# Second-layer weights four rows to a partition, first-layer columns at a step of four, five fetch buffers

## The chip, the core and the metric

The kernel runs on one core of a Trainium2 chip. The metric is the device time of one execution in microseconds. Before the change it is 216.29 us, the median of three runs (215.66 to 222.16).

## What is computed

Two layers follow each other. The first is an mLSTM cell: for 4 batches and 8 heads with a head size of 40, over 768 steps, with exponential input and forget gates that are kept stable by a running maximum `m`:

```
C = f_stab * C + i_stab * outer(v_t, k_t)
n = f_stab * n + i_stab * k_t
y_t = sigmoid(o_t) * (C @ q_t) / max(|n . q_t|, 1)
```

Its output, as 3072 rows of 320 values, goes into a mixture of 8 experts. Each row goes to one expert, and no row is dropped:

```
expert_idx = argmax(x @ w_gate);  gate_w = softmax(x @ w_gate)[expert_idx]
h = max(x_rows_of_e @ w1[e], 0)      # 320 -> 1024
y = gate_w * (h @ w2[e])             # 1024 -> 320
```

## The kernel before

**Recurrent stage.** The sequence of each batch is cut into 6 chunks of 128 steps, so there are 24 tiles, handled in one loop over `s` with an order that is written out by hand. A tile's rows are scored against the eight columns of `w_gate`, ranked, and scattered by GpSimd (`send`, L596) into a table `x_sorted` in device memory that is sorted by expert.

**Expert stage.** It starts in the last steps of the loop (at about 117 us in the trace) and takes the rest of the time. The rows of an expert are worked on in groups: a group of two tiles (256 rows) and a group of one tile (128 rows) for every expert, in the order of the list `order` (L824). Two groups, those of experts 0 and 1 with two tiles, are done early, while the buffers of the recurrent stage are still in place. Rows beyond the 384 of an expert go into five extra one-tile groups, whose expert is known only at run time. A loop of the same kind stands behind them for rows beyond these; it isn't entered where five extra groups are enough.

For a group, `turn` transposes its rows into `xT` (L253, L254), `layer1` computes the hidden values and applies the maximum with 0 (VectorE L286, ScalarE L288), and `layer2` computes the output `zp` (L293), copies it to `zo` (ScalarE, L298) and scatters it to the output rows (GpSimd, L300).

**Weights.** They lie in device memory as f32 and are cast to bf16 by the transfer itself, which GpSimd issues: `weights_whole` (L186) and `weights_half` (L193) for the first layer, `weights_out` (L200) for the second. All experts stay in two tiles, `w1_all` and `w2_all`. The program's transfers from GpSimd share eight completion semaphores in turn, so one waits until the eighth before it has landed.

**The layout that the change touches.** A block of 128 hidden values is one contraction of the second layer. Which 128 of the 1024 rows of `w2[e]` form a block is free, so long as the first layer computes the same hidden values in that block. With `j=2`, partition `p` holds the rows 2p and 2p+1 of a stretch of 256, which lie next to each other in device memory. Block `fb` then has every second hidden value, so the first layer reads the columns of its weights at a step of two. These lines say it:

```python
w2_all[:, e].rearrange("p e (a j) d -> p (e a) (j d)", j=2)            # L201
return fb // 2 * 256 + fb % 2                                          # L257
lhsT=w[:, c : c + 255 : 2], rhs=xT[:, db, :]                           # L282
```

The columns are the operand of the weight load (LDWEIGHTS), 24 of them a group: 8 at L271 over 64 partitions and 16 at L280 over 128.

**Fetches.** An extra group can't name its expert's weights when the program is built. So `fetch` (L808 to L813) copies them from `w1_all` and `w2_all` into buffers `wx1` and `wx2`, issued on SyncE's queue with the expert's number in a register. There are `XW` buffers of each; fetch number `x` is issued when group `i = 14 - XW + x` starts (L841 to L843). Since a fetch may read any expert, the first of them waits until all weights have landed.

**PSUM banks of the early groups.** The recurrent stage has six tags with one bank each (`tk`, `tq`, `sA`, `sB`, `dC`, `xt`) and one tag, `hp`, with two. `spots` (L624 to L629) says which bank the early expert groups use for what; a list is used in turn. Their outputs `zp` have the two banks of `hp`.

Of the kernel before, what the change touches and what calls it, by code (L numbers as in the profile page):

```python
# [19 lines left out]
def kernel(  # L20
# [37 lines left out]
    FL = DB - 1  # L58
# [10 lines left out]
    XU = 5  # L69
    NE = 2  # L70
    PE_ = 7
    XW = 4
    NV = 6
    NS = N + 128

# [89 lines left out]
    w2_all = big.tile([128, E, FB, Dm], BF16)  # L165
# [32 lines left out]
    def weights_out(e0, n):  # L198
        e = slice(e0, e0 + n)
        nc.gpsimd.dma_start(  # L200
            w2_all[:, e].rearrange("p e (a j) d -> p (e a) (j d)", j=2),  # L201
            moe_w2[e].rearrange("e (a p j) d -> p (e a) (j d)", p=128, j=2),
        )

    def apart(ins, group):
# [24 lines left out]
    def spot(kind, shape, dtype):  # L230
        i = turns[kind] = turns.get(kind, -1) + 1
        at = spots[kind][i % len(spots[kind])]
        if isinstance(at, tuple):
            tag, pool = at
            return pool.tile(shape, dtype, name=kind, tag=tag)[:]
        n = 1
        for m in shape[1:]:
            n *= m
        at = at[:, :n]
        return at.rearrange("p (a b) -> p a b", b=shape[2]) if len(shape) == 3 else at  # L240
# [13 lines left out]
        nc.vector.tensor_copy(g["xT"], tp)  # L254

    def column(fb):
        return fb // 2 * 256 + fb % 2  # L257

    def layer1(g, u):
        n = g["n"]  # L260
        per = 4 // n
        w, xT = g["w"][0], g["xT"]
        v = u // 2 * per
        if u == 0:
            g["h"] = spot("h", [128, FB, n * 128], BF16)
            g["hp"] = [spot("hp", [128, per, n * 128], F32) for _ in range(2 * n)]
            for k in range(HF):
                for a in range(2):
                    c = FL * F + column(k)
                    r = slice(64 * a, 64 * a + 64)  # L270
                    nc.tensor.matmul(  # L271
                        g["hp"][k // per * 2 + a][:, k % per, :], lhsT=w[r, c : c + 255 : 2], rhs=xT[r, FL + a, :],
                        start=(k % per == 0), stop=False, skip_group_check=True,
                    )
        a = u % 2
        hp = g["hp"][u]
        for i in range(per):
            for db in range(FL):
                c = db * F + column(a * HF + v + i)
                nc.tensor.matmul(  # L280
                    hp[:, i, :], lhsT=w[:, c : c + 255 : 2], rhs=xT[:, db, :], start=False, stop=(db == FL - 1),
                    skip_group_check=True,  # L282
                )
        dst = g["h"][:, a * HF + v : a * HF + v + per, :]
        if a == 0:
            nc.vector.tensor_relu(dst, hp)  # L286
        else:
            nc.scalar.activation(dst, hp, AF.Relu)  # L288
# [30 lines left out]
    with tc.tile_pool(name="ring", bufs=1) as ring_pool, \  # L319
# [301 lines left out]
        for i in range(1, NV):  # L621
            pads(i)
        early = [dict(e=e, n=NE, k=0, si=0, zp="zp") for e in range(2)]
        spots.update(  # L624
            hp=[(t_, ps1) for t_ in ("sA", "sB", "tk", "tq")], tp=[("dC", ps1)], zp=[("hp", ps2)],
            h=[kq[:, i].rearrange("p a h d -> p (a h d)").bitcast(BF16) for i in range(2)],
            xT=[kq[:, 2, a].rearrange("p h d -> p (h d)").bitcast(BF16) for a in range(2)],
            zo=[zo_e[:, i, :] for i in range(4)],
# [6 lines left out]
        for s in range(-3, NT):  # L635
# [55 lines left out]
            if s == NT - 5:  # L691
                weights_out(0, 1)
            if s == NT - 4:
                weights_in(1, 1)
            if s == NT - 3:
                weights_out(1, 1)
            if s == NT - 2:
                weights_in(2, 1)
        weights_whole(3)
        assert sent == NT - 4  # L700
        layer1(first, 0)
        xtrans(NT - 1)
        gate(P0)
        rank(P0, NT - 1)
        layer1(first, 1)
        place(P0)
        for t in (NT - 4, NT - 3):
# [3 lines left out]
        logits(P0 + 1, NT)  # L711
        choose(P0 + 1)
        layer1(first, 2)
        gate(P0 + 1)
        targets(1, 0)
# [8 lines left out]
        nc.vector.tensor_copy(tot[:], rt[P0 + 1]["tot"])  # L724
        weights_half(3)
        weights_out(2, 1)
        weights_out(3, 1)
        layer2(first, 0)
# [79 lines left out]
    def fetch(ex):  # L808
        wx1 = wk_pool.tile([128, FL * F + F // 2], BF16, name="wx1", bufs=XW)
        wx2 = wk_pool.tile([128, FB, Dm], BF16, name="wx2", bufs=XW)  # L810
        nc.sync.dma_start(wx1[:], w1_all[:, bass.ds(ex, 1), :].rearrange("p e b -> p (e b)"))
        nc.sync.dma_start(wx2[:].rearrange("p a b -> p (a b)"), w2_all[:, bass.ds(ex, 1)].rearrange("p e a b -> p (e a b)"))  # L812
        return wx1, wx2  # L813

    def expert_of(x):
        return nc.sync.value_load(xe[0:1, bass.ds(x, 1)], min_val=0, max_val=E - 1)
# [22 lines left out]
    for i, g in enumerate(groups):  # L839
        nw = g.get("e", E) + 3  # L840
        x = i - len(order) + XW  # L841
        if 0 <= x < XU:
# [21 lines left out]
    with tc.If(nx > XU):  # L864
        with tc.For_i(XU, nx, 1) as i:
            iv = wk_pool.tile([128, 1], F32, name="iv")
            nc.vector.tensor_copy(iv[:], invx[:, bass.ds(i, 1)])
            g = dict(n=1, w=fetch(expert_of(i)), apart=False)
# [36 lines left out]
```

## Time and profile before

The profile covers one execution with a span of 205.5 us on the one core, at a mean granted TensorE clock of 0.992.

| engine | busy us | share of the span |
|---|---|---|
| TensorE, matmuls | 184.8 | 90% |
| TensorE, weight loads (beside the matmuls) | 153.1 | 75% |
| VectorE | 125.5 | 61% |
| ScalarE | 117.0 | 57% |
| GpSimd | 142.0 | 69% |

| transfers | count | size of one, as written | median time from issue to landing |
|---|---|---|---|
| second-layer weights, GpSimd's queue | 8 | 640.0 KB | 8.7 us |
| first-layer weights, whole part | 8 | 512.0 KB | 10.6 us |
| first-layer weights, half part | 16 | 64.0 KB | 8.4 us |
| fetches of the extra groups, SyncE's queue | 10 | 640.0 KB | 7.0 us |

How to read it: matmuls are pipelined and their ends are modelled, so a TensorE that is 90% busy isn't at 90% of its peak. The sizes of cast transfers are those of the bf16 side; twice as many bytes are read. In the views of the trace a line names the source line, the engine, the operation, and the tiles as `written<-read`; `w_all` stands for `w1_all` and `w2_all`, `wx` for `wx1` and `wx2`. PEld is the weight load of TensorE; SPq is SyncE's queue.

### The profile page before, as it was taken

What the parts mean: (1) busy time and instruction counts of PE and PEld (TensorE: products, weight loads), DVE (VectorE), ACT (ScalarE), POOL (GpSimd) and SP (SyncE); (2) the same over time, 40 slices, a digit from 0 to 9 for tenths busy, and PEclk for the clock granted to TensorE, in tenths of its full rate; (3) what the DMA queues carried; (4) which work ended last, traced back from release to release, by engine and by line L of the source; (5) the groups of instructions that cost most, each with busy time, mean ns of one, the idle gap of its engine ahead of it and who ended that gap; (6) DMA issues with size and microseconds to landing.
All of it is one profiled execution on the core that took longest, in us unless ns stands there. A gap on an engine that the chain in (4) does not pass through costs nothing.

```text
span 205.5 us, 5756 instructions
## 1 busy us (share of the span) xinstructions
PE 184.8 (90%) x2055; PEld 153.1 (75%) x2055; DVE 125.5 (61%) x410; ACT 117.0 (57%) x273; POOL 142.0 (69%) x259
## 2 busy tenths in 40 slices
PE   1289999999999999999999999998998999999660
PEld 1166888888999989998888877666866877777450
DVE  7854757678777887879858774454853343433210
ACT  1457775878978988699584375343333342533320
POOL 6024779546486898978899978974437769898632
PEclk9999999999999999999999999999999999999996
DMA  7999999999999899999969998999999999999930
GB/s 137 197 190 192 208 225 193 190 226 206 217 172 212 165 188 185 199 185 192 199 93 280 254 222 188 122 210 249 234 233 217 228 263 273 393 378 389 366 133 23
DMA packets 116686, 44.32 MB, mean 216 GB/s; under 512 B 102506, under 2 KB 111725, under 8 KB 116656
## 3 DMA queue, kind: packets, MB, share of 16 engines
q1 hardware_dynamic: 105456, 25.34, 59.1%
q0 software_dynamic: 10736, 18.38, 40.4%
q8 instruction: 17, 0.28, 0.5%
q10 hardware_dynamic: 464, 0.21, 0.4%
q14 instruction: 13, 0.11, 0.1%
HBM read 39.30 MB, written 9.37 MB: 237 GB/s over the span
## 4 chain that ended last, share of the span: by engine, by line
PE 44%; DMA 21%; DVE 9%; POOL 8%; issue 7%; ACT 5%; SPq 4%; POOLq 1%; ACTq 0%; DVEq 0%
DMA w_all<-in_moe_w_dram 18%; PE hp L418 7%; PE hp L486 7%; PE tk L380 5%; PE dC L426 5%; PE sA L393 4%; PE tq L380 4%; PE xt L463 4%; PE sA L398 3%; POOL out_dram L300 3%; DMA wx<-w_all 2%; PE hp L438 2%; SPq L812 2%; POOL w_all L193 2%; POOL rest L309 2%
## 5 line engine op out<-in xcount | busy, mean ns | idle before, releaser
L286 DVE TENSOR_SCALAR h<-hp 128x512 bf16<-128x512 f32 x25 | 17.3, 692 | 35.2 <-PE hp L280 16.4
L288 ACT ACTIVATE h<-hp 128x512 bf16<-128x512 f32 x25 | 14.9, 597 | 25.5 <-PE hp L280 24.1
L596 POOL DMA_INDIRECT x_sorted<-x_all,slots x24 | 25.5, 1061 | 5.3 <-issue 3.1
L456 POOL TENSOR_TENSOR x_sb<-x_sb,den 128x320 f32<-128x320 f32 x23 | 16.7, 726 | 15.8 <-DVE den L454 15.3
L300 POOL DMA_INDIRECT out_dram<-zo,s_idx x20 | 19.9, 994 | 7.1 <-ACT zo L298 3.1
L293 PE MATMUL zp<-w_all,h 128*128 128x320 bf16 x160 | 24.0, 299 | 0.7 <-DMA w_all<-in_moe_w_dram 0.7
L293 PEld LDWEIGHTS <-h 128*128 128x128 bf16 x200 | 18.8, 98 | 7.1 <-DMA w_all<-in_moe_w_dram 0.9
L405 ACT CAST dB<-sB 128x512 bf16<-128x512 f32 x24 | 14.0, 584 | 14.0 <-PE sB L399 12.7
L280 PEld LDWEIGHTS <-w_all 128*128 128x128 bf16 x256 | 18.9, 98 | 3.7 <-issue 1.3
L298 ACT COPY zo<-zp 128x320 f32<-128x320 f32 x25 | 10.6, 425 | 18.4 <-PE zp L293 18.4
L418 PE MATMUL hp<-C_sb,qT 104*128 104x82 f32 x160 | 20.7, 272 | 0.1
L380 PE MATMUL tk<-ident,kq 128*104 128x128 f32 x96 | 16.7, 300 | 4.1 <-DMA kq<-in_k_dram 4.1
L280 PE MATMUL hp<-xT,w_all 128*128 128x128 bf16 (+1 forms) x224 | 20.1, 243 | 0.0
L418 PEld LDWEIGHTS hp<-C_sb,qT 104*128 104x128 f32 x160 | 19.4, 192 | 0.6 <-PE tq L380 0.3
L368 POOL CAST vAb<-vA 128x328 bf16<-128x328 f32 x24 | 11.0, 460 | 11.7 <-DVE vA L366 11.7
L465 ACT COPY xT<-xt 128x384 f32<-128x384 f32 x24 | 11.6, 482 | 12.4 <-PE xt L463 12.1
L406 POOL TENSOR_SCALAR_AFFINE_SELECT dB<-dB 128x512 bf16<-128x512 bf16 x24 | 16.5, 689 | 2.2 <-ACT dB L405 2.0
L426 PE MATMUL dC<-vA,kq 128*104 128x82 f32 x160 | 17.9, 255 | 0.0
L486 PE MATMUL hp<-wg_sb,xT 128*128 128x8 f32 x144 | 17.7, 256 | 0.0
L403 DVE TENSOR_TENSOR dA<-sA,cmask 128x512 bf16<-128x512 f32 x24 | 16.0, 667 | 1.9 <-PE sA L398 1.9
L486 PEld LDWEIGHTS hp<-wg_sb,xT 128*128 128x128 f32 x144 | 17.0, 192 | 0.0
L426 PEld LDWEIGHTS dC<-vA,kq 128*104 128x104 f32 x160 | 16.3, 172 | 0.0
(156 smaller groups left out, 454.8 us busy)
## 6 DMA issues: line engine op xcount, KB each, us to landing
wx<-w_all SPq DMA_DIRECT2D x10, 640.0 KB, 7.0
w_all<-in_moe_w_dram POOLq DMA_DIRECT2D x8, 640.0 KB, 8.7
w_all<-in_moe_w_dram POOLq DMA_DIRECT2D x8, 512.0 KB, 10.6
kq<-in_k_dram SPq DMA_DIRECT2D x24, 160.0 KB
kq<-in_q_dram SPq DMA_DIRECT2D x24, 160.0 KB
v<-in_v_dram SPq DMA_DIRECT2D x24, 160.0 KB, 3.8
o_sb<-in_o_gate_dram SPq DMA_DIRECT2D x24, 160.0 KB
x_sorted<-zrow POOLq DMA_DIRECT2D x8, 241.5 KB, 3.5
```

What stands on the lines that cost most here:

```text
L280: nc.tensor.matmul(hp[:, i, :], lhsT=w[:, c : c + 255 : 2], rhs=xT[:, db, :], start=False, stop=(db == FL - 1), skip_group_check=True,)
L286: nc.vector.tensor_relu(dst, hp)
L293: nc.tensor.matmul(zp, lhsT=g["h"][:, fb, j * 128 : (j + 1) * 128], rhs=g["w"][1][:, fb, :], start=(fb == 0), stop=(fb == FB - 1),)
L300: ins = nc.gpsimd.indirect_dma_start(out=out[:, :], out_offset=bass.IndirectOffsetOnAxis(ap=at, axis=0), in_=zo, in_offset=None, bounds_ch ...
L380: nc.tensor.transpose(tp[:, j, :], two(d[n], j), ident[:])
L403: nc.vector.tensor_tensor(d["dA"][:], sA[:], cmask[:, None, :].to_broadcast([128, PR, 128]), op=ALU.mult)
L406: nc.gpsimd.affine_select(d["dB"][:], d["dB"][:], compare_op=ALU.is_ge, fill=0.0, base=0, pattern=[[0, PR], [1, 128]], channel_multiplier=-1,)
L418: nc.tensor.matmul(hp[:, 2 * j * D1 : (2 * j + 2) * D1], lhsT=d["qT"][:, j, :], rhs=st["C"][:, j].rearrange("p h d -> p (h d)"), start=(j ...
L426: nc.tensor.matmul(st["dC"][:, j], lhsT=two(d["k"], j), rhs=d["vA"][:, 2 * j : 2 * j + 2, :], start=(c == 0 and j == 0), stop=True, skip_g ...
L456: eng.tensor_tensor(x3d, x3d, den[:].unsqueeze(2).to_broadcast([128, H, D]), op=ALU.mult)
L486: nc.tensor.matmul(lg[:, i * E : (i + 1) * E], lhsT=st[t]["xT"][:, db * 128 : (db + 1) * 128], rhs=wg_sb[:, db, :], start=(fresh and i == ...
L596: ins = nc.gpsimd.indirect_dma_start(out=xs[:, :], out_offset=bass.IndirectOffsetOnAxis(ap=slots[:, t : t + 1], axis=0), in_=x_all[:, t, : ...
```

## The change

It has four parts. The second-layer weights are laid out with four neighbouring rows to a partition, so that a piece of the transfer is twice as long. The first layer's columns are read at a step of four, which keeps the blocks of both layers matched. The fetch buffers go from four to five, so that each of the five extra groups has its own. And the two outputs of the second early group go to the banks of `dC` and `xt`, while the first early group keeps those of `hp`.

```diff
-    XW = 4
+    XW = 5
...
-            w2_all[:, e].rearrange("p e (a j) d -> p (e a) (j d)", j=2),
-            moe_w2[e].rearrange("e (a p j) d -> p (e a) (j d)", p=128, j=2),
+            w2_all[:, e].rearrange("p e (a j) d -> p (e a) (j d)", j=4),
+            moe_w2[e].rearrange("e (a p j) d -> p (e a) (j d)", p=128, j=4),
...
     def column(fb):
-        return fb // 2 * 256 + fb % 2
+        return fb // 4 * 512 + fb % 4
...
-    lhsT=w[r, c : c + 255 : 2], rhs=xT[r, FL + a, :],
+    lhsT=w[r, c : c + 509 : 4], rhs=xT[r, FL + a, :],
...
-    lhsT=w[:, c : c + 255 : 2], rhs=xT[:, db, :], start=False, stop=(db == FL - 1),
+    lhsT=w[:, c : c + 509 : 4], rhs=xT[:, db, :], start=False, stop=(db == FL - 1),
...
-            hp=[...], tp=[("dC", ps1)], zp=[("hp", ps2)],
+            hp=[...], tp=[("dC", ps1)], zp=[("hp", ps2), ("hp", ps2), ("dC", ps1), ("xt", ps1)],
```

More of the change, by code (lines that the diff above doesn't have):

```diff
@@ L271, in layer1 @@
                     nc.tensor.matmul(
-                        g["hp"][k // per * 2 + a][:, k % per, :], lhsT=w[r, c : c + 255 : 2], rhs=xT[r, FL + a, :],
+                        g["hp"][k // per * 2 + a][:, k % per, :], lhsT=w[r, c : c + 509 : 4], rhs=xT[r, FL + a, :],
                         start=(k % per == 0), stop=False, skip_group_check=True,
@@ L280, in layer1 @@
                 nc.tensor.matmul(
-                    hp[:, i, :], lhsT=w[:, c : c + 255 : 2], rhs=xT[:, db, :], start=False, stop=(db == FL - 1),
+                    hp[:, i, :], lhsT=w[:, c : c + 509 : 4], rhs=xT[:, db, :], start=False, stop=(db == FL - 1),
                     skip_group_check=True,
@@ L624 @@
         spots.update(
-            hp=[(t_, ps1) for t_ in ("sA", "sB", "tk", "tq")], tp=[("dC", ps1)], zp=[("hp", ps2)],
+            hp=[(t_, ps1) for t_ in ("sA", "sB", "tk", "tq")], tp=[("dC", ps1)], zp=[("hp", ps2), ("hp", ps2), ("dC", ps1), ("xt", ps1)],
             h=[kq[:, i].rearrange("p a h d -> p (a h d)").bitcast(BF16) for i in range(2)],
```

## Prediction

> **What bounds the kernel now.** I read first the page's slices, since the change touches transfers and matmuls. These two lines give the busy tenths of TensorE and of the 16 DMA engines in 40 slices of 5.14 us:
>
> ```profile
> PE   1289999999999999999999999998998999999660
> ...
> DMA  7999999999999899999969998999999999999930
> ```
>
> Both look full, so busy shares don't tell which one sets the end. I went on to the table by stretches (columns: busy us and instruction count of each engine, granted clock, DMA share, GB/s), for the expert stage, from 112 us on:
>
> ```profile
> 112.00:130.00 18.00, 17.41 (x182) 14.08 (x181) 11.41 (x46) 8.87 (x25) 15.51 (x28) 1.00 1.03 209
> 130.00:148.00 18.00, 16.83 (x181) 12.54 (x181) 10.29 (x29) 6.28 (x13) 11.39 (x17) 1.00 1.12 213
> 148.00:166.00 18.00, 17.14 (x196) 12.80 (x194) 7.94 (x22) 6.93 (x14) 9.92 (x16) 1.00 1.15 238
> 166.00:175.00 9.00, 9.00 (x98) 7.04 (x97) 3.94 (x9) 3.19 (x7) 7.86 (x13) 1.00 1.12 262
> 175.00:196.00 21.00, 18.88 (x248) 14.38 (x245) 7.63 (x21) 8.00 (x16) 17.01 (x26) 1.00 0.99 377
> ```
>
> The DMA share is about 1 or above throughout (above 1 means that packet records overlap), and TensorE is a little short of full in all but one stretch. The chain of waits for 112 to 206 us (start, length, what) says which comes last:
>
> ```profile
> 134.99 14.86 DMA w_all<-in_moe_w_dram
> ...
> 151.19 14.40 DMA w_all<-in_moe_w_dram
> ...
> 166.39 8.67 DMA w_all<-in_moe_w_dram
> ...
> 175.07 0.49 SPq L812
> ...
> 183.25 5.13 DMA wx<-w_all
> ```
>
> The weights of the experts arrive one behind another until 175.07. Only then may the fetches (L811, L812) run, because they read an expert chosen at run time and so wait for all weights. The timeline of TensorE shows what that costs it (last bracket: idle before, and who ended it):
>
> ```profile
> 130.39 0.61 PE L253 MATMUL tp<-ident_b,x_all 128*128 128x128 bf16 x8 [0.51 <-ACT zo_e L298]
> ...
> 140.95 0.31 PE L293 MATMUL zp<-w_all,h 128*128 128x320 bf16 x1 [0.69 <-DMA w_all<-in_moe_w_dram]
> ...
> 154.12 0.28 PE L271 MATMUL hp<-xT,w_all 64*128 64x256 bf16 x1 [0.30 <-DMA w_all<-in_moe_w_dram]
> 154.96 0.28 PE L271 MATMUL hp<-xT,w_all 64*128 64x256 bf16 x2 [0.56 <-DMA w_all<-in_moe_w_dram]
> ...
> 195.75 0.40 PE L271 MATMUL hp<-xT,wx 64*128 64x128 bf16 x8 [2.12 <-DMA wx<-w_all]
> ```
>
> So a byte stream sets the end: six experts' weights from 128 to 175 us, five experts' fetches from 175 to 196, and the last group of rows, which can't begin until its fetched weights land at 195.75. TensorE is close behind, with 0.51 + 0.69 + 0.30 + 0.56 + 2.12 = 4.18 us of such waits in all. What follows 195.75 is 9.7 us of fixed tail.
>
> [...]
>
> **Second-layer weights, four rows to a partition (L201, L202).** The transfer of one expert was 512 pieces of 2,560 B read (1,280 written as bf16); it becomes 256 pieces of 5,120 read (2,560 written). The packet records of the software queue give the mean time of a piece on its DMA engine: 108.3 ns for 2,048 B read (L193), 122.6 for 2,560 (L200 now), 177.7 for 4,096 (L186). From the last two the slope is 55.1 ns per 1,536 B, so 5,120 B take 122.6 + 91.8 = 214.4 ns. Two pieces now take 245.1. Each pair saves 30.7 ns; 256 pairs on 16 engines are 16 each, 0.49 us an expert. Records overlap by 1.15 there, so 0.43 us of time. The weights of experts 2 to 7 move inside the saturated stretch: 6 x 0.43 = 2.6 us. Those of experts 0 and 1 come earlier, and GpSimd's issue of expert 2's at 128.38, which follows the row scatters, doesn't hang on them, so they count nothing. Bounds: with medians (116 and 172 ns) it is 0.36 an expert, 1.9 us in all; if the fixed part is that of the fit through 2,048 and 4,096 B (38.9 ns) and overlap is not divided out, 3.7 us; if the wire limits and not the pieces, 0. I take 2.5. Issue on GpSimd hardly changes: 0.81 us an issue here, 0.77 for L186 with 256 pieces.
>
> **Columns at a step of four (L256, L272, L282).** The same loads in the same order; only the stride differs. The rows of groups of like shape (mean ns after the bar's first comma):
>
> ```profile
> L280 PEld LDWEIGHTS <-w_all 128*128 128x128 bf16 x256 | 18.9, 98 | 3.7 <-issue 1.3 <-DMA out_dram<-zo,s_idx 0.2 <-DMA w_all<-in_moe_w_dram 0.2
> L293 PEld LDWEIGHTS <-h 128*128 128x128 bf16 x200 | 18.8, 98 | 7.1 <-DMA w_all<-in_moe_w_dram 0.9
> ...
> L486 PEld LDWEIGHTS hp<-wg_sb,xT 128*128 128x128 f32 x144 | 17.0, 192 | 0.0
> ```
>
> Step two (L280) costs what step one (L293) costs. Lower bound 0. Upper bound: the load runs like the f32 one, 192 ns. Its pairs of load and matmul pace at 1.33 us / 12 = 111 ns; pairs of L280 on 128 rows pace at (1.07 - 0.22) / 15 = 57 ns. The 13 one-tile groups have 16 such pairs each: 208 x 54 ns = 11.2 us. Two-tile groups pace at about 113 ns ((1.92 - 0.22) / 15) and hide it. I take 0[...].
>
> **Five fetch buffers (L72, L809, L843).** Each fetch of the fifth expert no longer waits until the first one's buffers are read: 0.4 us at L811 and 0.8 at L812 in SP's waits, with nothing queued behind but that fetch. I cost it at nothing: the other fetches and scatters hide it, since DMA moves 385 to 405 GB/s in each microsecond from 185 to 188, and the order of the fetches stays. At most 1.2 us. No wait is added.
>
> **Early outputs on other PSUM banks (L625).** The second expert's two outputs go to the banks of dC and xt in place of hp. The transposes at 130.39 then needn't wait for the copy of zo_e: 0.51 us of TensorE, before a wait for bytes. In return the first matmuls of the next group wait for that copy, which ends at 130.33, before they are due. Off the path, 0.
>
> **Sum.** Bytes land 2.5 us earlier. TensorE gets back up to 0.51 + 0.69 + 0.86 = 2.06 us before the last fetch, so it would be ready at 193.63 - 2.06 = 191.6, and the fetch lands at 195.75 - 2.5 = 193.2: bytes still bound. 216.3 - 2.5 = 213.8 us.
>
> **Rivals.** First, TensorE becomes the bound: pieces cost more than the means say, or the early fetch closes gaps. All 4.18 us go: 212.1, and a little less where unprofiled runs, about 9 us longer than the profiled one (216.3 against 207.2), lose more to transfers. For it: the upper bound of 3.7 plus part of 1.2. Against: it needs both. Second, the wire is the limit: weights read about 400 GB/s already, as do fetches with 5,120-byte pieces, which have 208.5 ns a piece; then 216. Against: the 122.6 and 177.7 ns. Third, slower: loads at step four pace at 111 ns. TensorE then bounds, 212.1 + 11.2 = 223.3 us. [...] Against: steps one and two are alike.
>
> **How the numbers follow.** Forecast 0.48, TensorE-bound 0.28, wire 0.10, slow loads 0.14. The last lies outside the range with a little of the second's low end. The range goes from 210.0 (the second with more lost waits in the longer unprofiled runs) to 218.0 (the wire case with noise, or loads a little slower). Faster by over 2% means under 211.96: most of the second case and a tail of the first, 0.30. Slower: 0.15. Within: 0.55.
>
> **What would show it.** Right: records of 5,120 B read near 214 ns; the last weight transfer lands near 172.5; L280 loads stay at 98 ns; the wait at L271 for the last fetch is still there, near 1.6 us. Wrong: loads well above 98 ns or a pace above 57; two records per 5,120 B; or no wait for the last fetch, which makes it the second case.

## The result and the profile after

The changed kernel took 221.94 us in the median of four runs (220.47 to 222.34), against 215.97 us for the kernel before in the same comparison. The ratio is 1.0289, with an interval of 1.0207 to 1.0371. It is slower; the forecast was 213.8. Some executions of one kernel are several us longer than others, at a lower granted clock (before_again: 226.15 us at 0.938, 212.13 at 0.989), so ratios and intervals, here and below, are of the faster ones alone, while medians and ranges count all.

The spans of the two profiles are 220.1 and 205.5 us. The 40 slices of the changed kernel (5.5 us each) show the first hint, at their right end:

```profile
PE   1299999999999999989979999999899746999600
...
DMA  7999999999998999999999969999999999951100
```

There are two new things. TensorE has a dip (7, 4, 6) near 180 us, and then two whole slices with nothing on it, with hardly a transfer beside them. The table by stretches, with the columns of before, says the same in microseconds:

```profile
130.00:148.00 18.00, 17.66 (x187) 13.78 (x185) 9.97 (x29) 6.57 (x13) 12.41 (x19) 1.00 1.06 208
148.00:166.00 18.00, 17.13 (x193) 13.35 (x193) 8.28 (x22) 6.87 (x14) 10.07 (x16) 1.00 1.11 240
166.00:175.00 9.00, 7.77 (x89) 6.23 (x86) 3.23 (x7) 2.51 (x5) 7.86 (x13) 1.00 1.10 231
175.00:196.00 21.00, 15.62 (x166) 12.11 (x162) 5.33 (x13) 5.65 (x12) 11.52 (x18) 0.84 0.97 384
...
212.00:220.00 8.00, 0.00 (x0) 0.00 (x0) 0.00 (x0) 0.00 (x0) 0.00 (x0) 0.50 0.00 0
```

In the last row no engine works and no byte moves for 8 us. Everything is done, and the execution doesn't end. Busy shares can't say who holds it, because instructions that only wait, count or drain aren't counted as busy. The view of one line, for the last line of the program and GpSimd's queue, does (operation, count, then ns as min/median/max, and first and last start in us). First before, then after:

```profile
L900 POOLq DRAIN  x3: 46/109/737, 203.5 to 205.2; - x3
```

```profile
L900 POOLq DRAIN  x3: 46/109/7665, 211.6 to 219.8; - x3
```

A drain at the end of GpSimd's program took 0.74 us and now takes 7.67. One instruction ahead of it, INC_SWDGE_SEM, has grown too; I call it the count of the transfer queue. The same view for its line, before and after:

```profile
L864 POOLq INC_SWDGE_SEM  x1: 332/332/332, 203.1 to 203.1; - x1
```

```profile
L864 POOLq INC_SWDGE_SEM  x1: 2032/2032/2032, 209.5 to 209.5; - x1
```

Together these two went from 1.07 to 9.70 us, 8.6 us more. From the start of the count to the end of the span it is 2.4 us before and 10.6 after, so the span is 8.2 us longer by it.

The rest of the difference of the spans, 203.1 to 209.5, is mainly one stop of TensorE. The timeline of TensorE after (in brackets: idle before, and who ended it):

```profile
183.69 0.62 PE L271 MATMUL hp<-xT,w_all 64*128 64x128 bf16 x8 [4.89 <-DVE xT L254]
```

The granted clock is 0.50 from 182 to 188 us, so TensorE also works at about half pace for some 4 us after the stop: 16 matmuls of L280 take 1.90 us from 184.25, and 1.08 from 189.80. The 0.84 in the table holds this. After the stop no group waits for a fetch any more. The stop looks like a part of the loss, but it isn't one of the change: the unchanged kernel, profiled again, has it as well (experiment 1).

### The profile page after: what moved, and what is told of

Same layout as the page of the kernel before. It is cut to its first block, busy times and chain, and to the rows that moved or that the text cites. A ratio compares the mean times of both kernels' runs of the same rounds, so it can differ in the third digit from the quotient of the medians.

```text
span 220.1 us, 5745 instructions
## 1 busy us (share of the span) xinstructions
PE 187.1 (85%) x2046; PEld 157.5 (72%) x2055; DVE 125.9 (57%) x410; ACT 117.0 (53%) x273; POOL 141.9 (64%) x259
## 3 DMA queue, kind: packets, MB, share of 16 engines
q0 software_dynamic: 8688, 18.38, 35.9%
## 4 chain that ended last, share of the span: by engine, by line
PE 46%; DMA 16%; DVE 9%; issue 7%; POOL 6%; SPq 5%; ACT 4%; POOLq 1%; ACTq 0%
DMA w_all<-in_moe_w_dram 8%; PE hp L486 7%; PE hp L418 6%; PE hp L280 5%; PE tk L380 4%; DMA wx<-w_all 4%; PE zp L293 4%; DMA o_sb<-in_o_gate_dram 4%; PE dC L426 4%; PE tq L380 3%; PE xt L463 3%; POOL out_dram L300 3%; PE sA L398 3%; PE sA L393 3%; SPq L812 2%
## 5 line engine op out<-in xcount | busy, mean ns | idle before, releaser
L293 PE MATMUL zp<-w_all,h 128*128 128x320 bf16 x160 | 25.0, 306 | 0.2 <-DMA w_all<-in_moe_w_dram 0.2
L280 PEld LDWEIGHTS <-w_all 128*128 128x128 bf16 x256 | 21.4, 117 | 2.4 <-issue 1.6
L280 PE MATMUL hp<-xT,w_all 128*128 128x128 bf16 (+1 forms) x224 | 21.1, 250 | 0.0
L405 ACT CAST dB<-sB 128x512 bf16<-128x512 f32 x24 | 14.0, 584 | 12.8 <-PE sB L399 10.6
L368 POOL CAST vAb<-vA 128x328 bf16<-128x328 f32 x24 | 11.1, 460 | 11.7 <-DVE vA L366 11.7
L366 DVE TENSOR_TENSOR vA<-v,G_T 128x328 f32<-128x328 f32 x24 | 15.6, 648 | 1.4 <-issue 1.4
```

Source lines behind the costliest of these rows:

```text
L280: nc.tensor.matmul(hp[:, i, :], lhsT=w[:, c : c + 509 : 4], rhs=xT[:, db, :], start=False, stop=(db == FL - 1), skip_group_check=True,)
L293: nc.tensor.matmul(zp, lhsT=g["h"][:, fb, j * 128 : (j + 1) * 128], rhs=g["w"][1][:, fb, :], start=(fb == 0), stop=(fb == FB - 1),)
```

## The experiments

The first theory: the layout has fewer pieces in GpSimd's transfer queue (packet records 10,736 before, 8,688 after), and the end depends on what has gone through that queue. Its rivals: loads at step four, or one of the other parts of the change, cost the time.

Unless said otherwise, a comparison stands against runs of the kernel before on the same chip. "End" is the count plus the drain, in ns.

### 1. The unchanged kernel again, and each part alone

```diff
--- before_again: no edit
--- w2_only, against before
-    j=2
+    j=4                                    # L201, L202
-    return fb // 2 * 256 + fb % 2
+    return fb // 4 * 512 + fb % 4
-    lhsT=w[r, c : c + 255 : 2]
+    lhsT=w[r, c : c + 509 : 4]             # L272, L282
--- xw5_only, against before
-    XW = 4
+    XW = 5
--- zp_only, against before
-    zp=[("hp", ps2)],
+    zp=[("hp", ps2), ("hp", ps2), ("dC", ps1), ("xt", ps1)],
```

> The unchanged kernel, for a second profile. Theory A (the 8.9 us in which VectorE and ScalarE get TensorE's results late at 172 to 183 us come from the change) expects no idle of VectorE over 4 us between 170 and 190 us, and TensorE's last group at about 196. Theory B (that hold-up and the 7.7 us of GpSimd's last drain befall any execution) expects one or both here too. Either expects a timed ratio of 1.00; a drain near 7.7 us in this profile would say that the first profile of before, at 207.2 us, was 7 us short of what the timed runs usually have.

> The layout of four rows to a partition and the columns at a step of four alone; four fetch buffers and the old PSUM banks. If the layout is the cause of the loss: ratio near 1.03. If the hold-up comes from the five fetches queued at once: no hold-up, ratio 0.99 to 1.00, with loads of 115 ns in place of 98 and at most 0.03 us more a group.

> Five fetch buffers alone. If the five fetches queued at once hold up the other engines: ratio 1.02 to 1.03 and an idle of VectorE over 4 us between 170 and 190 us. If the layout is the cause, or chance: ratio 1.00 and no such idle.

> The other PSUM banks for the second early group's outputs alone. All theories expect 0 to 0.5 us less, a ratio of 1.00; the wait of the transposes for the copy of zo_e, 0.51 us at 130 us, is gone.

| kernel | median us (lowest to highest) | ratio to before, interval | end |
|---|---|---|---|
| before_again | 215.63 (212.13 to 226.15) | 1.0001 (0.991 to 1.0093) | 332 + 732 |
| w2_only | 225.04 (223.11 to 237.02) | 1.045 from two runs, no interval | 2032 + 7665 |
| xw5_only | 216.53 (212.25 to 232.35) | 0.9989 (0.9942 to 1.0037) | 332 + 739 |
| zp_only | 214.43 (211.83 to 218.42) | 0.9887 (0.9782 to 0.9993) | 332 + 739 |

The layout alone brings a loss of that size and the whole long end, to the nanosecond; the view of the last line in w2_only:

```profile
L900 POOLq DRAIN  x3: 46/109/7665, 213.1 to 221.3; - x3
```

The fifth buffer does nothing that can be measured. The banks may bring a little: the interval just leaves out 1, but the ratio rests on two runs of zp_only, so that is not shown.

The timeline of TensorE in the unchanged kernel, profiled again, has the stop:

```profile
188.27 0.51 PE L271 MATMUL hp<-xT,w_all 64*128 64x128 bf16 x8 [5.24 <-issue]
```

It is 4.9 us in w2_only, 5.0 in zp_only, 6.5 in xw5_only, and absent from the first profile of before and from a second one of the changed kernel (after_again, experiment 3). So it comes with the execution and not with the change. It is one part of why that first profiled run, of 207.2 us, was shorter than the other runs of the same kernel. It isn't all: in before_again, whose span is 11.7 us longer, GpSimd issues the second-layer weights of expert 2 at 135.56 in place of 128.38, 7.2 us later and long before the stop.

### 2. Is it the step of the columns?

The second-layer rows stay four to a partition, but the columns are read at a step of two, so the hidden values of a block no longer match the rows of `w2` that they meet.

```diff
--- w2_step2, against before
-    j=2
+    j=4                                    # L201, L202 only
```

> The transfers of the second-layer weights with four rows to a partition, but the first layer's columns still at a step of two, so that the hidden values of a block and the rows of the second layer's weights no longer match; the amount of work is the same. Transfer theory (GpSimd's end, 2.0 us of the queue's count and 7.7 us of drain in place of 0.3 and 0.7, comes from the other number or length of the pieces): the long end is here, near 9.7 us, and the loads are back at 98 ns. Column theory (it comes with the step of four): short end, 1.1 us.

It took 227.65 us (224.82 to 237.31), on a chip on which the kernel before took 229.84 (219.44 to 234.32), so the time says little. The profile says what is needed. The groups of instructions by line (busy us and mean ns after the bar), first after, then w2_step2:

```profile
L280 PEld LDWEIGHTS <-w_all 128*128 128x128 bf16 x256 | 21.4, 117 | 2.4 <-issue 1.6 <-DMA out_dram<-zo,s_idx 0.2
...
L271 PEld LDWEIGHTS <-w_all 64*128 64x128 bf16 x128 | 5.6, 115 | 11.5 <-issue 9.8 <-DMA w_all<-in_moe_w_dram 1.4 <-DMA x_sorted<-x_all,slots 0.3
```

```profile
L280 PEld LDWEIGHTS <-w_all 128*128 128x128 bf16 x256 | 19.6, 101 | 3.8 <-issue 1.7 <-DMA out_dram<-zo,s_idx 0.2
```

The loads are back at about 100 ns, and the end is still 2032 + 7665. The long end doesn't hang on the step.

### 3. Fill the queue again, or empty it

Small transfers of 256 pieces of 16 bytes (written), into a tile that nobody reads, are added to GpSimd's queue in the steps of the recurrent stage. Eight bring back the 2,048 pieces that the layout took away. In the other direction, the eight transfers that clear the sorted table leave GpSimd's queue for SyncE's.

```diff
--- after_more8 and after_more8_b (the same kernel), against after
--- more8_four: also XW = 4; after_more4, after_more7: 4 or 7 in place of the last 8
--- before_more8: the same lines, against before
+    pad_sb = rte.tile([128, 8, 2, 8], BF16)
...
+        def more(i):
+            nc.gpsimd.dma_start(pad_sb[:, i], moe_w2[i, 0:256, 0:8].rearrange("(p a) d -> p a d", a=2))
...
+            if E <= s < E + 8:
+                more(s - E)
--- before_clear_sp, against before
-            nc.gpsimd.dma_start(xs[...], zrow[:])
+            nc.sync.dma_start(xs[...], zrow[:])
```

> The changed kernel with 8 small transfers from GpSimd added in the recurrent stage, 256 pieces of 8 values each, so that its queue has as many pieces as before the change. Count theory (the long end depends on how many pieces the queue has had): the end is back at 1.1 us, and the time falls by 8 to 9 us to 212 to 214, ratio 0.97 to 0.99. Length theory (pieces of 5,120 bytes cause it): end still 9.7 us, ratio 1.03.

> The same with 4 added transfers, 1,024 pieces. Count theory: an end that differs from 9.7 us, between it and 1.1 us if it is in proportion, or one of the two if it is a threshold. Length theory: 9.7 us.

> The kernel before with the 8 added transfers, so its queue has 2,048 pieces more than before. Count theory: an end that may be other than 1.1 us, since the position in the queue is another; length theory: 1.1 us.

> The changed kernel again, on the same chip as the next three. Count theory: an end of 9.7 us (2.0 of the queue's count, 7.7 of drain), ratio 1.02 to 1.03.

> The changed kernel with the 8 added transfers, again, to be compared with the changed kernel on one chip. Count theory: an end of 1.2 us and 7 to 9 us less than the changed kernel, so a ratio to the kernel before of 0.985 to 0.995, the gain of the layout that the long end hid. If the layout has no gain of its own: 1.00. If the changed kernel's loss has another cause: 1.02.

> The same with four fetch buffers. If the fifth buffer is worth nothing, as the prediction has it: the same time within 0.5%.

> The kernel before, with the 8 clearing transfers (128 pieces each) issued from SyncE's queue in place of GpSimd's; nothing else moves. By my count GpSimd's queue then has 957 entries on each DMA engine, in place of 1,029. Count theory with a step between 969 and 1,029: a long end of about 10 us in a kernel that has nothing of the change, ratio 1.03 to 1.04. Any theory that ties the long end to the layout of the second-layer weights: 1.1 us and a ratio of 1.00.

| kernel | median us (lowest to highest) | before there | ratio, interval | end |
|---|---|---|---|---|
| after_more8 | 220.5 (218.68 to 220.83) | 229.84 (219.44 to 234.32) | none | 363 + 805 |
| after_more4 | 231.82 (one run) | 229.84 | none | 2123 + 7992 |
| before_more8 | 217.45 (one run) | 229.84 | none | 643 + 1948 |
| after_again | 225.22 (222.39 to 235.3) | 216.86 | 1.0359 (1.0265 to 1.0454) | 2032 + 7665 |
| after_more8_b | 215.89 (212.0 to 226.29) | 216.86 | 0.9943 (0.9889 to 0.9997) | 364 + 805 |
| more8_four | 215.02 (212.19 to 225.0) | 216.86 | 0.9892 (0.9799 to 0.9986) | 364 + 805 |
| before_clear_sp | 224.93 (221.62 to 227.98) | 216.86 | 1.0294 (1.0208 to 1.0381) | 1872 + 7012 |

The last four stand side by side on one chip. In the view of the last line, after_more8_b has the changed layout and a short end; before_clear_sp has the old layout, step and buffers and a long one:

```profile
L906 POOLq DRAIN  x3: 46/109/805, 208.2 to 209.9; - x3
```

```profile
L900 POOLq DRAIN  x3: 46/109/7012, 217.3 to 224.9; - x3
```

So the end follows what has gone through the queue, whichever kernel it is in. Its removal takes the changed kernel's ratio from 1.0359 to 0.9943, about 9 us, for 8.5 us of end. The count theory was less exact than that. The end of after_more4, 10.1 us, was expected at 9.7 or less, that of before_clear_sp, 8.9, at about 10. And on the first chip, where before itself ranged from 219.44 to 234.32 us, after_more8 took 220.5 and not 212 to 214.

The time of before_clear_sp isn't the end's alone. SyncE, which has loads of its own to issue, issues the last clear at 60.9 us, and GpSimd's first scatter waits until 66.13, where in the kernel before it starts at 57.75. The timeline of before_clear_sp (idle before, in brackets):

```profile
66.13 1.18 POOL L596 DMA_INDIRECT x_sorted<-x_all,slots  x1 [9.11 <-DMA kq<-in_q_dram]
```

For it the drain is the evidence and the ratio is not.

Whether the added transfers cost time of their own isn't shown. The last product of the recurrent stage (the view of its line, last number the last start) comes later with them than in the first profile after, but on their own chip it comes later still without them. First after, then after_again, then after_more8_b:

```profile
L426 PE MATMUL dC<-vA,kq x160: 234/255/255, 18.1 to 112.3; 128*104 128x82 f32 x160
```

```profile
L426 PE MATMUL dC<-vA,kq x160: 234/255/381, 18.3 to 119.4; 128*104 128x82 f32 x160
```

```profile
L427 PE MATMUL dC<-vA,kq x160: 234/255/255, 18.4 to 117.0; 128*104 128x82 f32 x160
```

The same kernel has 112.3 us in one execution and 119.4 in another, so the 4.7 us between after and after_more8_b can't be laid to the transfers. Of more8_four, with four buffers, it is shown that it doesn't have the changed kernel's loss (0.9892 against 1.0359). That it is faster than the kernel before is not: its upper bound, 0.9986, is close to 1, and the ratio rests on three runs. What the layout itself would bring without a long end and without added transfers was not tried.

### 4. Where the step lies

The first form of the theory: the length restarts where a count of entries passes 1,024, a guess between 969 (after_more4, long) and 1,029 (before, short). The count is an estimate of mine. For each of the 16 DMA engines I take one entry for 16 pieces, and one more for every transfer, since the packet records of this queue have 1,488 of 4 bytes in before as in after, 16 for each of 93 transfers. That gives 1,029 before, 901 after. In the last two kernels each step adds two transfers of 1,024 pieces to the kernel before.

```diff
--- before_wide7, before_wide8 (8 for 7 in the last condition), against before
+    pad_sb = rte.tile([128, 8, 8, 2, 8], BF16)
...
+        def more(i):
+            for c in range(2):
+                nc.gpsimd.dma_start(pad_sb[:, i, :, c], moe_w2[i, :, 160 * c : 160 * c + 8].rearrange("(p a) d -> p a d", a=8))
...
+            if E <= s < E + 7:
+                more(s - E)
```

> The changed kernel with 7 of the 8 added transfers. By my count GpSimd's queue then has 1,020 entries on each DMA engine, where 8 gave 1,037 and a short end. If the length of the end starts again at every 1,024 entries: a long end of about 10 us. If the step lies lower, between 969 and 1,020: a short end near 1.1 us.

> The kernel before with 14 small transfers of 1,024 pieces of 8 values added, 1,939 entries by my count. If the end starts again at every 1,024 entries: 915 entries into the second stretch, so about 9 to 11 us. If the end is long only below a threshold: short, and at most 3 us as with 1,165 entries.

> The same with 16 such transfers, 2,069 entries. If the end starts again at every 1,024: 21 entries into the third stretch, about 1.2 us. If it grows with all that the queue has had past the threshold: 10 us or more.

One run each, beside before at 219.32 us: after_more7 226.04 us with an end of 2183 + 8237; before_wide7 223.4 with 743 + 2357; before_wide8 224.47 with 983 + 3337. The first agreed: at 1,020 entries the end is still long, at before's 1,029 short. The other two fell outside both forms, before_wide7 only just outside the second (3.1 us, where at most 3 was expected). Nor does the amount in the queue alone order the ends: 957 entries (before_clear_sp) ended sooner than 901, and 2,069 far sooner than either.

### 5. A rule that fits, and its trial

Across the long ends the drain grows by 82 ns for each transfer, those of 128 pieces (from 85 to 93) and those of 256 (from 93 to 100) alike: 85 transfers 7012, 93 transfers 7665, 97 transfers 7992, 100 transfers 8237. Read the other way, the short ends are those of 8, 9, 23, 28 and 40 transfers. Going through the transfers in program order gives these numbers with one rule. Add up their entries. When a transfer takes the sum past about 1,024, only that transfer and the seven before it stay in the sum. With n transfers in the sum at the end, the count takes about 172 + 20 n ns and the drain 73 + 81.6 n ns. This is an estimate, arithmetic fitted to the nine ends; the traces show transfers, pieces and durations, and not what GpSimd holds or does in them. The expectations below call the 1,024 the room, and a transfer that takes the sum past it the first that doesn't fit. Seven is also the number of transfers between two that share one of the eight semaphores (numbers 111 to 118 in turn, over all 93 transfers in the trace of before); whether that is the reason was not tried.

A rule with that many numbers, made after nine ends, needs ends that it hasn't seen:

```diff
--- before_more4: the lines of experiment 3 with 4 in place of the last 8, against before
--- four_wide2, four_wide3 (3 for 2 in the last condition), against more8_four
-    pad_sb = rte.tile([128, 8, 2, 8], BF16)
+    pad_sb = rte.tile([128, 3, 8, 8], BF16)
...
-            nc.gpsimd.dma_start(pad_sb[:, i], moe_w2[i, 0:256, 0:8].rearrange("(p a) d -> p a d", a=2))
+            nc.gpsimd.dma_start(pad_sb[:, i], moe_w2[i, :, 0:8].rearrange("(p a) d -> p a d", a=8))
...
-            if E <= s < E + 8:
+            if E <= s < E + 2:
```

> New theory, fitted to nine earlier ends: [...] 172 + 20 n ns for its queue count and 73 + 81.6 n ns for its drain. Here the transfer that ends at entry 1,025 is the first not to fit; eight follow it, so n = 16: count 492 ns (490 to 530), drain 1,379 ns (1,370 to 1,385). If the room is 1,025 or more, the next one is the first: n = 15, drain 1,297. Rival (the end follows the amount in the queue, between 1,037 entries with 805 ns and 1,165 with 1,948): drain near 1,340 with no reason to hit 1,379, so this run alone does not refute it; the next two do.

> Changed kernel with four fetch buffers and two transfers of 1,024 tiny pieces in place of eight of 256: 95 transfers, 1,031 entries. The theory: the last transfer is the first that does not fit, so n = 8: count 332 ns, drain 726 to 739 ns, time as the eight small ones gave, 0.985 to 0.995 of before, since two issues fewer than eight cost GpSimd less but each has more pieces. Rival (amount in the queue): between 1,029 and 1,037 entries, 332 to 364 and 735 to 805, hardly another answer; what this run adds is whether the repair works with other transfers.

> The same with three such transfers: 96 transfers, 1,096 entries. The theory: one transfer ends exactly at entry 1,024 and still fits if the room is 1,024; the next is the first that does not, seven follow it, n = 15: count 472 ns (470 to 510), drain 1,297 ns (1,290 to 1,302). If the room is under 1,024, n = 16 and the drain 1,379. Rival (the end follows the amount in the queue): 1,096 entries is one less than before_more4 has, so the drain would be the same as there within 10 ns. The theory says 82 ns less.

The view of the last line, for before_more4, four_wide2 and four_wide3 in this order:

```profile
L906 POOLq DRAIN  x3: 46/109/1377, 216.6 to 218.6; - x3
```

```profile
L906 POOLq DRAIN  x3: 46/109/738, 233.3 to 234.9; - x3
```

```profile
L906 POOLq DRAIN  x3: 46/109/1377, 227.0 to 228.9; - x3
```

The counts were 503, 351 and 499 ns. The rule's drains of 1,379 and 726 to 739 were met; its count of 332 for four_wide2 was 19 ns short. For four_wide3 the value for a room under 1,024 came, 1,377, so a sum of 1,024 already counts as past the limit, and 1,020 (after_more7) doesn't. With that put right, the rule gives all twelve contents of the queue within 13 ns of drain and 19 ns of count. But four_wide3 was the run that was to part it from the rival, and the rival had forecast the same there. Past 1,024 entries the ends do rise with the amount, in very uneven steps: the 68 entries from 1,097 to 1,165 add 571 ns of drain, the next 774 only 409. The rule gives these steps, a rise with the amount doesn't say why; but no forecast made ahead sets the two apart. So it is shown that the end depends on what went through the queue, and the rule is a description that fits.

As a repair, two wide transfers failed: four_wide2 took 229.06 us (226.78 to 239.17) against 226.77 (219.04 to 231.22) for before on that chip, ratio 1.0323 (1.0205 to 1.0441), with a short end. The forecast was 0.985 to 0.995. Its profile is of an execution of 236.88 us at a clock of 0.905, with the last product of the recurrent stage at 133.3 us, 16 us later than in after_more8_b. That can't be laid to the two transfers: before_wide8, with sixteen of this size, has that product at 124.7 us. Two further single runs were 220.58 (before_more4) and 230.9 us (four_wide3). Where four_wide2 loses its time stays open.

## Why the prediction was wrong, step by step

**The step that failed** is the sentence "What follows 195.75 is 9.7 us of fixed tail." It isn't fixed. Within it lie GpSimd's count and drain, 1.07 us of no engine's busy time, which the change made 9.70. No term of the sum, no bound and no rival stood for it. I had seen that the software queue would have fewer pieces, and asked only what a piece costs on its DMA engine. By the fitted rule, the kernel before passes the limit only with its very last transfer (1,029 entries), so 8 of 93 transfers are in the sum at the end; with 128 entries fewer it never does, and all 93 are. Seen so, the old kernel's short end was luck that the new layout used up.

**The bound** was read rightly, though it doesn't show in the first profile after. There TensorE's stop lets the fetches get ahead (the last is issued at 186.9 us, TensorE starts the last group at 203.33), and no group waits for one: the sign that the prediction had named for TensorE as the bound. In after_again, after_more8_b and more8_four, which haven't the stop, the last groups wait for fetched weights; in after_again, the changed kernel itself, the last one waits 1.88 us at 204.12 (forecast near 1.6). The timeline of TensorE in after_more8_b has the same:

```profile
195.85 0.42 PE L272 MATMUL hp<-xT,wx 64*128 64x128 bf16 x8 [1.05 <-DMA wx<-w_all]
200.36 0.42 PE L272 MATMUL hp<-xT,wx 64*128 64x128 bf16 x8 [1.76 <-DMA wx<-w_all]
```

**The layout's gain**, the 2.5 us of the sum, was too large, and may be nothing. The records of 5,120 B had a mean of 219.2 ns in the first profile (median 209; forecast 214.4 and by medians 209.3), and 217.4 to 232.0 in the eleven profiles with this layout, 226.5 on average. A pair then saves 19 ns in place of 30.7, which by the same working is 1.6 us for six experts. On the path not even that shows. I forecast the last weight transfer to land near 172.5. The view of the fetch's line, for before and then after (first and last start), has the first fetch of `w2`, which waits for the last weights, at the same time:

```profile
L812 SPq DMA_DIRECT2D wx<-w_all x5: 486/1132/1788, 175.1 to 188.4; - x5
```

```profile
L812 SPq DMA_DIRECT2D wx<-w_all x5: 490/1227/1500, 175.1 to 186.9; - x5
```

In this profile GpSimd issues the weights of expert 2 later, at 129.61 in place of 128.38 us. From that issue to the end of the last weight record it is 45.1 us after and 46.3 before. Over all profiles it is 45.1 to 47.7 with the new layout (eleven, 46.1 on average) and 45.7 to 47.8 with the old (nine, 46.6): some 0.5 us of the forecast 2.5, within the spread. The timed loss fits: against 8.2 us of longer end, the ratios 1.0289, 1.0359 and w2_only's 1.045 are 6.2, 7.7 and 9.7 us, so no gain is shown. Why so little of what a piece saves reaches the path was not settled.

**Loads at step four**: costed at 0, nearly rightly, although they did slow down, which the prediction had named as a sign of being wrong. The zero rested on steps one and two, 98 ns each before; step four takes 117 over 128 partitions and, over 64, 115 in place of 95. Why it does was not tried. That a slower load costs next to nothing was an estimate, and shows in the pace of pairs on 128 rows, which went only from 56.7 to 57.3 ns (16 pairs in 1.07 us, then 1.08), and the last one-tile groups start 2.67 us apart in place of 2.64, an estimate of 0.6 us over 21 groups.

**Five buffers** at 0: right, 0.9989 alone. **Early outputs on other banks** at 0 on the path: the wait of 0.51 us is gone, since the transposes now follow without one in the timeline:

```profile
128.79 2.34 PE L293 MATMUL zp<-w_all,kq 128*128 128x320 bf16 x16
130.96 0.61 PE L253 MATMUL tp<-ident_b,x_all 128*128 128x128 bf16 x8
```

The ratio of zp_only, 0.9887 (0.9782 to 0.9993), leaves room for more than 0.51 us, or for nearly nothing.

**The rivals.** The third ended on the side that came, near its 223.3 us, and for another reason: it needed pairs at 111 ns, and they pace at 57. Agreement in the total would have hidden this.

## What to carry to other kernels

Look at what stands between the last useful instruction and the end of the span before calling it fixed, above all at GpSimd's drain (0.73 to 8.24 us here) when its transfers are changed in number, size or queue; busy tables don't show it. A change of layout that makes a queue's pieces fewer can lengthen the end, as here by 8.6 us. When a profiled run is much shorter than the timed ones, take a second profile before reading a gap as the change's doing.

## What was not expected of the hardware

- GpSimd's count and long drain at the end took together from 1.06 us (before_again) to 10.4 us (after_more7), and repeat closely for the same queue (2032 and 7665 in four profiles of three kernels, 332 and 732 to 739 in four of before, before_again, xw5_only and zp_only).
- Bf16 weight loads of 128 columns over 128 partitions took 98 to 104 ns at a column step of one or two, and 114 to 117 at four.
- Between 178 and 206 us TensorE stops for 4.5 us (after_more7) to 6.5 (xw5_only) in at least ten of the twenty profiles, of changed and unchanged kernels alike, and not in others (before, after_again, after_more8_b, more8_four). Its cause was not tried.
